# Turning the keys only with two banks free, and moving a sum and its flag away from the end of a packed-attention and expert kernel

## The chip, the cores and the metric

One core of a Trainium2 chip runs the program. The metric is the device time of one execution in microseconds. TensorE is called PE below, VectorE DVE, ScalarE ACT, GpSimd POOL and SyncE SP.

## The reference

Eight batches, eight heads of 576 positions and 64 features, 32 packs. The packs attend to keys and values, the queries attend to the packed result, and the concatenated heads (512 features) go through one of eight experts per token.

```python
def sm_attn(qq, kk, vv):
    s = scale * np.matmul(qq, kk.transpose(0, 1, 3, 2))
    s = s - np.max(s, axis=-1, keepdims=True)
    a = np.exp(s)
    a = a / (np.sum(a, axis=-1, keepdims=True) + 1e-09)
    return np.matmul(a, vv)
p_packed = sm_attn(p, k, v)
out = sm_attn(q, p_packed, p_packed)
...
        prev_e = -1
        for s in range(S):
            fresh_e = int(np.argmax(logits[b, s]))
            if s == 0 or local_gate[b, s] < 0.5:
                e = fresh_e
            else:
                e = prev_e if prev_e >= 0 else fresh_e
            prev_e = e
            ls = logits[b, s] - logits[b, s].max()
            p = np.exp(ls)
            p /= p.sum() + 1e-09
            h = np.maximum(x[b, s] @ w1[e], 0.0)
            out[b, s] = p[e] * (h @ w2[e])
```

Here x is the output of the attention, (8, 576, 512), w1 is 8 x 512 x 1024 and w2 is 8 x 1024 x 512.

## The kernel before

The kernel puts all tokens of a batch through the expert of the batch's first token. Tokens that would go elsewhere are called strays; they are counted, and only if there is one does a slow branch at the very end compute the batches again. With these inputs there is none.

For each batch a number of generators issue the work. `turn_keys` and `scores` make the products of packs and keys; `keys` takes the exponential of the scores (probabilities of the packs over the keys, two groups Q of four heads) and turns them: three transposes of 116 x 128 into one bank of PSUM, then two into another (line 573), each bank copied out to a1T (line 575, ACT). `packed_keys` multiplies them with the values (line 604). `queries` (lines 655 to 711) has the queries' attention, whose result is split into a2h and a2l, a high and a low part. `gates` (lines 918, 926) has the gate's logits, which DVE reads out of a bank turned (lt, line 933). `choose` reads the number of the expert into a register of SP, and `weights` then loads w1t (line 1021) and w2raw (line 1028).

The first layer's weights are multiplied with the packed result first: `pack_weights` (line 1065, two groups of eight products, two banks) gives wph (ACT's cast, line 1074) and wpl (DVE, line 1077) for four of the eight chunks of 128 hidden units. A chunk is then `layer1` in two halves of the tokens (line 1093: six products into one bank), `relu` (line 1104 on ACT, line 1109 on DVE, which gives the bank back), `split` of the second layer's weights (line 1120 on ACT, line 1124 on POOL) and `layer2`, in blocks of 128 tokens: 0 to 3 have three products each (line 1135), block 4 two (lines 1141, 1145). These add up in acc0 to acc4 over the eight chunks; then `store` scales and stores a block. PSUM has eight banks: five are the acc, and three, bank0 to bank2, serve everything else.

`chunks` is the main generator. It walks through the batches and chunks and puts the blocks of the chunk before between the halves of layer 1. Behind the last chunk of batch 7 stand the `tails`, the blocks of the last two chunks in six groups. All other generators are threads of `weave`, which picks whose step is issued next by a clock that it keeps of planned times. A `need(tiles, slot, banks)` tells that clock when a step could go on: when the tiles are written, and when that many of the three banks are free. It decides only the order in which instructions are issued; what they wait for on the chip are semaphores on the tiles and banks themselves, and every engine runs its own list in order.

`look_for_strays` sums the strays over the partitions with a 1 x 1 product (line 1193), casts the sum to an integer, `some` (line 1195, DVE), and loads it into a register on all five engines (line 1198), where the branch at the end reads it. `chunks` calls it ahead of the last chunk of batch 7 (line 1256).

Of the kernel before, what the change touches and what calls it, by code (L numbers as in the profile page):

```python
# [19 lines left out]
B, H, S, D = 8, 8, 576, 64  # L20
# [3 lines left out]
NQ = H // HQ  # L24
# [145 lines left out]
def packed_attn_moe_kernel(  # L170
# [33 lines left out]
    turns, banks, spare = [], [f"bank{x}" for x in range(3)], [f"acc{x}" for x in range(1, 4)]  # L204
# [54 lines left out]
    stray = const.tile([128, 1], F32, name="stray")  # L259
# [8 lines left out]
    def give(*tiles):  # L268
        clock.done.update(x.tensor.name for x in tiles)
# [5 lines left out]
    def need(*tiles, slot=(), banks=0, when=None, more=None, skip=()):  # L275
        slots = [(x, 1) if isinstance(x, str) else x for x in ((slot,) if isinstance(slot, str) else slot)]

        def ready():

            if (when is not None and not when()) or not all(clock.free_slot(*x) for x in slots):  # L280
                return None
            free = free_banks("front" if more == "front" else more is not None and lent(more), skip)
            if len(free) < banks:
                return None
            return max(clock.ready(tiles), free[banks - 1][0] if banks else 0.0, *(clock.slot(*x) for x in slots))
        ready.banks = banks
        return ready
# [259 lines left out]
    def keys(st, Q):  # L547

        yield need(when=lambda: ("nb", Q) in st and ("v", Q) in st)
        sc, nb = st["sc", Q], st["nb", Q]  # L550
        chunks_ = sc.rearrange("a (p c) -> a c p", c=NV)
        yield need(nb)
        s2 = tile_([128, 2], F32, "s2")
        if st["early"]:
            for r, t in enumerate(st["ts", Q]):
                nc.scalar.activation(
                    out=st["parts", Q][:, r], in_=t[:, :HALF].rearrange("a (c i) -> a c i", c=NT), func=AF.Exp,
                    bias=nb, scale=SCALE, accum_out=s2[:, r:r + 1],
                )
                give(t)  # L560
        else:
            nc.scalar.activation(out=sc[:, :S], in_=sc[:, :S], func=AF.Exp, bias=nb, scale=-1.0, accum_out=s2[:, 0:1])
        st["weighed"] += 1

        rooms = ("a1T", "a1U")
        yield need(s2, slot=rooms)
        a1T = [tile_([128, n, 128], F32, "a1T", room) for n, room in zip((J3, NV - J3), rooms)]
        for r, turned in enumerate(a1T):
            yield need(sc, banks=1)
            tp = bank()  # L570
            n = turned.shape[1]
            for j in range(n):
                nc.tensor.transpose(out=tp[:VP, 128 * j:128 * j + 128], in_=chunks_[:, J3 * r + j], identity=ident)  # L573
            copy = nc.vector.tensor_copy if st["early"] and (r == 1 or Q == 0) else nc.scalar.copy
            copy(out=turned[:VP], in_=tp[:VP, :128 * n].rearrange("a (j x) -> a j x", x=128))  # L575
            give(tp)
        give(sc)
        rs = tile_([128, 1], F32, "rs")
        if st["early"]:
            nc.vector.tensor_scalar(out=rs, in0=s2[:, 0:1], scalar1=s2[:, 1:2], scalar2=1e-9, op0=ALU.add, op1=ALU.add)  # L580
        else:
            nc.vector.tensor_scalar(out=rs, in0=s2[:, 0:1], scalar1=1e-9, scalar2=None, op0=ALU.add)
        nc.vector.reciprocal(out=rs, in_=rs)
        st["turned", Q] = a1T, rs
        if st["early"]:
            yield from packed_keys(st, (Q,))
        elif Q == NQ - 1:
            yield need(when=lambda: ("turned", 0) in st)
            yield from packed_keys(st, range(NQ))
# [452 lines left out]
    def pack_weights(st):  # L1042

        st["wp"], st["packed"], early = [], 0, st["early"]
        for fh in range(2):
            yield need(when=lambda: len(st.get("w1", ())) > fh and (
                (not st["first"] or (not fh or st["quads"] == NQ)) if not early else st.get("halved", 0) > 1 if fh else st["raised"] > 0
            ))
            pieces = st["w1"][fh]
            yield need(slot=("wph", "wpl"))  # L1050
            hi = tile_([128, NQ, 512], F32R, "wph")
            lo = tile_([128, NQ, 512], F32R, "wpl")
            for x in (hi, lo):
                clock.edges[x.tensor.name] = (256, 512, 768)
            st["wp"].append((hi, lo))
            width = 512 // len(pieces)
            for n, w1t in enumerate(pieces):
                cols = slice(width * n, width * n + width)
                skip = KEPT if early and fh == 0 else ()
                yield need(w1t, banks=NQ, skip=skip)  # L1060
                ts = [bank(skip=skip) for Q in range(NQ)]
                for Q in range(NQ):
                    rows = slice(64 * Q, 64 * Q + 64)
                    for h in range(HQ):
                        nc.tensor.matmul(  # L1065
                            out=ts[Q][32 * h:32 * h + 32, :width],
                            lhsT=st["ppT"][Q][rows, 32 * h:32 * h + 32],
                            rhs=w1t[rows, h],
                            start=True, stop=True,
                        )  # L1070
                if st["first"]:
                    yield need(*ts, when=lambda: not (early and n) or "cast" in st)
                for Q in range(NQ):
                    nc.scalar.copy(out=hi[:, Q, cols], in_=ts[Q][:, :width])  # L1074
                for Q in range(NQ):
                    yield need(hi[:, Q, cols], when=lambda: not early or ("back" in st if n == 0 else 0 in st["ready"]))
                    nc.vector.tensor_tensor(  # L1077
                        out=lo[:, Q, cols], in0=ts[Q][:, :width], in1=hi[:, Q, cols].bitcast(F32), op=ALU.subtract,
                    )
                give(*ts)  # L1080
                if n == len(pieces) - 1:
                    give(w1t)
                st["packed"] += width
# [103 lines left out]

    def look_for_strays():

        tc.mark_branch_hint_location("general", engines=list(engines_all))  # L1190
        yield need(stray, banks=1, when=lambda: "strays" in sts[B - 1])
        tot = bank()
        nc.tensor.matmul(out=tot[0:1, 0:1], lhsT=stray, rhs=ones_col, start=True, stop=True)
        some = sb.tile([1, 1], I32, name="some", bufs=1)
        nc.vector.tensor_copy(out=some, in_=tot[0:1, 0:1])  # L1195
        give(tot)
        yield need(some)
        found.append(nc.values_load(some[0:1, 0:1], min_val=0, max_val=128))

    def chunks(todo, aside, mask=None):  # L1200
# [40 lines left out]
        for b, st in todo:  # L1241
            tiles, begin_at = {}, 0
            if st["early"]:
                for c in range(FRONT):
                    yield from first(b, st, c, 0, tiles)
                for c in range(FRONT):
                    yield from second(tiles[c], (0, 1))
                for c in range(FRONT):
                    yield from first(b, st, c, 1, tiles)
                    if c:  # L1250
                        yield from second(tiles[c - 1], (2, 3, 4))
                last, begin_at = tiles[FRONT - 1], FRONT
            for c in range(begin_at, NC):
                end = c == NC - 1 and b is todo[-1][0]
                if end and mask is None:
                    yield from look_for_strays()
                for half, blocks in ((0, (0, 1, 2)), (1, (3, 4))):
                    yield from first(b, st, c, half, tiles)
                    if last is not None and not end:
                        done_before = (0, 1) if begin_at and c == begin_at else ()  # L1260
                        yield from second(last, tuple(x for x in blocks if x not in done_before))
                before, last = last, tiles[c]
# [12 lines left out]
        tails = ((before, (4, 0, 1)), (last, (4, 0)), (before, (2,)), (last, (1, 2)), (before, (3,)), (last, (3,)))  # L1275
        for n, (x, blocks) in enumerate(tails):
            yield from by_columns(x) if mask is None and n == 5 else second(x, blocks)

    def drain(*gs):
        for g in gs:  # L1280
# [58 lines left out]
    engines = mybir.EngineType  # L1339
    engines_all = (engines.PE, engines.Activation, engines.DVE, engines.Pool, engines.SP)  # L1340
    found = []
    sts = [dict() for _ in range(B)]
# [97 lines left out]
```

## Time and profile before

| | |
|---|---|
| time, median of 3 runs | 420.13 us (419.82 to 421.15) |
| time of the profiled execution | 420.32 us |
| its span, first to last instruction | 418.6 us |
| mean granted TensorE clock | 0.998 |
| PE busy | 406.5 us, 97% |
| DVE, ACT, POOL busy | 251.2, 189.4, 107.7 us |
| chain that ended last | PE 90%, DVE 5% |

The profile is of one execution. Busy times of PE overlap a little, since matmuls are pipelined; a timeline gives the start of each group of instructions, how long it took, and in brackets how long its engine had been idle and what ended that. The granted clock is full through all 40 slices of the page.

### The profile page before, as it was taken

Reading aid. Unit: us, or ns where it says so; the run is one execution under the profiler, and the core shown is the slowest. Engines: PE = TensorE matmul, PEld = TensorE weight load, DVE = VectorE, ACT = ScalarE, POOL = GpSimd, SP = SyncE. Lnnn points to the kernel's source line nnn. Section 1 sums busy time; section 2 is a strip of 40 time slices with the busy share of each in tenths; the row PEclk is TensorE's granted clock in tenths of the full one; section 3 lists DMA queues with packets and bytes.
Section 4 is the critical chain, followed back from the end, with each engine's and each line's share of the span. In section 5 each row is a group of like instructions: output and inputs, shape, how many; then the busy total and the mean of one; then the engine's idle time right before and its main releaser. Section 6 shows DMA issues by size and latency. Waiting matters only on the chain.

```text
span 418.6 us, 9782 instructions
## 1 busy us (share of the span) xinstructions
PE 406.5 (97%) x3724; PEld 317.3 (76%) x3725; DVE 251.2 (60%) x665; ACT 189.4 (45%) x447; POOL 107.7 (26%) x125
## 2 busy tenths in 40 slices
PE   8989999999999999999999999999999999999994
PEld 6776677777777887678768886788868887788873
DVE  4598388865865777578723886348842695432121
ACT  2574425643536452646353454535453552352232
POOL 1024022121341243113412252122512144213220
PEclk9999999999999999999999999999999999999999
DMA  8789979926994896699699706499191305430003
GB/s 232 239 305 230 170 237 251 226 83 154 337 185 160 187 173 187 241 205 207 224 295 187 221 9 237 156 210 240 32 349 32 122 13 206 172 121 18 2 1 117
DMA packets 161053, 72.98 MB, mean 174 GB/s; under 512 B 131186, under 2 KB 139882, under 8 KB 161002
## 3 DMA queue, kind: packets, MB, share of 16 engines
q1 hardware_dynamic: 160858, 72.19, 66.9%
q8 instruction: 30, 0.49, 0.5%
q14 instruction: 21, 0.17, 0.1%
q10 hardware_dynamic: 144, 0.13, 0.1%
HBM read 62.87 MB, written 9.44 MB: 173 GB/s over the span
## 4 chain that ended last, share of the span: by engine, by line
PE 90%; DVE 5%; ACT 1%; DMA 1%; issue 1%; SPq 0%; DVEq 0%; ACTq 0%
PE acc L1135 41%; PE bank L1093 25%; PE bank L1065 4%; PE acc L1141 4%; PE acc L1145 3%; PE bank L604 2%; PE bank L655 2%; PE bank L516 2%; PE bank L573 2%; PE acc L228 1%; DMA w1k<-in_moe_w_dram 1%; PE bank L918 1%; PE acc L445 1%; ACT wph L1074 1%; DVE h L1109 1%
## 5 line engine op out<-in xcount | busy, mean ns | idle before, releaser
L1135 PE MATMUL acc<-w2s,h 128*128 128x512 f32 (+1 forms) x771 | 204.2, 397 | 0.0
L1135 PEld LDWEIGHTS acc<-w2s,h 128*128 128x128 f32 x771 | 135.6, 188 | 31.6 <-issue 10.0
L1124 POOL TENSOR_TENSOR w2s<-w2raw,w2s 128x512 fp32r<-128x512 f32 (+1 forms) x68 | 85.4, 1259 | 249.3 <-ACT w2s L1120 229.8
L1109 DVE SCALAR_TENSOR_TENSOR h<-bank,h 128x224 fp32r<-128x224 f32 (+2 forms) x191 | 61.0, 347 | 86.5 <-ACT h L1104 85.3
L1104 ACT ACTIVATE h<-bank 128x288 fp32r<-128x288 f32 (+2 forms) x127 | 52.4, 413 | 111.4 <-PE bank L1093 101.8
L1093 PEld LDWEIGHTS bank<-a2h,wph 128*128 128x128 f32 x254 | 45.1, 188 | 22.8 <-issue 2.8
L1093 PE MATMUL bank<-a2h,wph 128*128 128x288 f32 (+2 forms) x254 | 57.8, 309 | 3.2 <-DVE wpl L1077 0.9
L1093 PE MATMUL bank<-a2l,wph 128*128 128x288 f32 (+2 forms) x254 | 54.5, 296 | 0.0
L1093 PE MATMUL bank<-a2h,wpl 128*128 128x288 f32 (+2 forms) x254 | 54.3, 295 | 0.0
L1093 PEld LDWEIGHTS bank<-a2h,wpl 128*128 128x128 f32 x254 | 40.9, 188 | 0.0
L1093 PEld LDWEIGHTS bank<-a2l,wph 128*128 128x128 f32 x254 | 40.7, 188 | 0.0
L1120 ACT CAST w2s<-w2raw 128x512 fp32r<-128x512 f32 x64 | 39.4, 616 | 1.8 <-DVE some L1195 1.6
L1077 DVE TENSOR_TENSOR wpl<-bank,wph 128x512 fp32r<-128x512 f32 (+1 forms) x32 | 20.6, 666 | 22.5 <-ACT wph L1074 22.5
L1141 PE MATMUL acc<-w2s,h 128*128 128x512 f32 x64 | 26.3, 411 | 0.0
L1145 PE MATMUL acc<-w2s,h 128*64 128x512 f32 x64 | 25.3, 396 | 0.0
L1074 ACT CAST wph<-bank 128x512 fp32r<-128x512 f32 (+1 forms) x32 | 16.8, 577 | 16.2 <-PE bank L1065 16.2
L1175 ACT ACTIVATE o<-acc,pe 128x512 f32<-128x512 f32 x23 | 15.8, 689 | 9.6 <-PE acc L1135 9.5
L711 POOL TENSOR_TENSOR a2l<-a2t,a2h 128x576 fp32r<-128x576 f32 x12 | 17.2, 1433 | 10.1 <-PE acc L1145 8.4
L640 DVE STREAM_TRANSPOSE qn<-qn 128x1152 f32<-128x1152 f32 x14 | 18.9, 1364 | 0.0
L673 DVE STREAM_TRANSPOSE sT<-bank 128x288 f32<-128x288 f32 x28 | 11.9, 462 | 11.3 <-ACT gate L671 10.0
L575 ACT COPY a1T<-bank 116x384 f32<-116x384 f32 (+1 forms) x28 | 11.5, 430 | 12.4 <-PE bank L573 12.3
L1065 PE MATMUL bank<-w1t,ppT 64*32 64x512 f32 x240 | 16.3, 601 | 0.0
(193 smaller groups left out, 403.0 us busy)
## 6 DMA issues: line engine op xcount, KB each, us to landing
w2raw<-in_moe_w_dram SPq DMA_DIRECT2D x64, 256.0 KB, 5.0
w1t<-in_moe_w_dram SPq DMA_DIRECT2D x15, 1024.0 KB, 5.2
kv<-in_v_dram SPq DMA_DIRECT2D x16, 560.0 KB, 7.6
qn<-in_q_dram SPq DMA_DIRECT2D x28, 288.0 KB, 4.6
out_dram<-o SPq DMA_DIRECT2D x31, 256.0 KB, 2.8
qn<-in_k_dram SPq DMA_DIRECT2D x24, 288.0 KB, 3.9
raw<-in_k_dram SPq DMA_DIRECT2D x4, 576.0 KB, 4.4
raw<-in_q_dram SPq DMA_DIRECT2D x2, 576.0 KB
```

The source lines that it names most:

```text
L640: nc.vector.transpose(out=qT, in_=qT)
L1065: nc.tensor.matmul(out=ts[Q][32 * h:32 * h + 32, :width], lhsT=st["ppT"][Q][rows, 32 * h:32 * h + 32], rhs=w1t[rows, h], start=True, stop= ...
L1074: nc.scalar.copy(out=hi[:, Q, cols], in_=ts[Q][:, :width])
L1077: nc.vector.tensor_tensor(out=lo[:, Q, cols], in0=ts[Q][:, :width], in1=hi[:, Q, cols].bitcast(F32), op=ALU.subtract,)
L1093: nc.tensor.matmul(out=t[:, :width], lhsT=st["wp"][c // 4][wi][:, Q, fs], rhs=a2[ai][Q][:, ts], start=(n == 0), stop=(n == 5),)
L1104: nc.scalar.activation(out=h[:, lo:hi], in_=t[:, :hi - lo], func=AF.Relu)
L1109: nc.vector.scalar_tensor_tensor(out=h[:, dst:dst + z - a], in0=t[:, a:z], scalar=0.0, in1=h[:, lo + a:lo + z].bitcast(F32), op0=ALU.max, ...
L1120: nc.scalar.copy(out=w[:, 0], in_=raw)
L1124: rest.tensor_tensor(out=w[:, 1, cols], in0=raw[:, cols], in1=w[:, 0, cols].bitcast(F32), op=ALU.subtract)
L1135: nc.tensor.matmul(out=acc[:, cols], lhsT=hs[hi], rhs=w[:, wi, cols], start=(c == 0 and n == 0), stop=(n == 2 and (c == NC - 1 or c == NC ...
L1141: nc.tensor.matmul(out=acc, lhsT=h[:, 512:S + TAIL], rhs=w[:, 0], start=(c == 0), stop=False, skip_group_check=True,)
L1145: nc.tensor.matmul(out=acc[0:TAIL], lhsT=h[:, 512:S], rhs=w[:, 1], start=False, stop=(c == NC - 1), skip_group_check=True,)
```

## The change

A turn of the keys waits in the planner's clock for two free banks (NQ is 2) in batches 1 to 7, where it was one. The strays' product and cast are issued in `pack_weights` of batch 7, right ahead of its second and last pack, when three banks are free, and the loads into registers become a function of their own, called behind the third group of the tails.

```diff
         for r, turned in enumerate(a1T):
-            yield need(sc, banks=1)
+            yield need(sc, banks=1 if st["early"] else NQ)
             tp = bank()
...
                 skip = KEPT if early and fh == 0 else ()
+                if isinstance(st["b"], int) and st["b"] == B - 1 and fh:
+                    yield need(w1t)
+                    yield from look_for_strays()
                 yield need(w1t, banks=NQ, skip=skip)
...
     def look_for_strays():
 
-        tc.mark_branch_hint_location("general", engines=list(engines_all))
-        yield need(stray, banks=1, when=lambda: "strays" in sts[B - 1])
+        yield need(stray, banks=NQ + 1, when=lambda: "strays" in sts[B - 1])
         tot = bank()
         nc.tensor.matmul(out=tot[0:1, 0:1], lhsT=stray, rhs=ones_col, start=True, stop=True)
         some = sb.tile([1, 1], I32, name="some", bufs=1)
         nc.vector.tensor_copy(out=some, in_=tot[0:1, 0:1])
         give(tot)
+        found.append(some)
+
+    def load_found():
+
+        some = found.pop()
+        tc.mark_branch_hint_location("general", engines=list(engines_all))
         yield need(some)
         found.append(nc.values_load(some[0:1, 0:1], min_val=0, max_val=128))
 
...
-                if end and mask is None:
-                    yield from look_for_strays()
...
             yield from by_columns(x) if mask is None and n == 5 else second(x, blocks)
+            if mask is None and n == 2:
+                yield from load_found()
```

Lines behind the first edit of `pack_weights` have numbers that are higher by 3 after the change (L1065 becomes L1068, L1093 becomes L1096, L1135 becomes L1138), those at the end by 8.

The first place is PE's order where batch 1's keys are turned (a1_477 and a1_659 are the two groups' probabilities; the numbers behind a bank count its uses). Before:

```order
L573 MATMUL bank1_696<-ident_72,a1_477 116x128 x3
L573 MATMUL bank2_702<-ident_72,a1_477 116x128 x2
L1093 MATMUL bank1_713<-a2h_120,wph_457 128x320
...
L1135 MATMUL acc2_726<-w2s_538,h_537 128x512 x3
L1065 MATMUL bank2_732<-w1t_397,ppT_226 32x512 x4
L1065 MATMUL bank0_733<-w1t_397,ppT_226 32x512 x4
L573 MATMUL bank1_751<-ident_72,a1_659 116x128 x3
L1135 MATMUL acc3_758<-w2s_538,h_537 128x512 x3
L1141 MATMUL acc4_762<-w2s_538,h_537 128x512
L1145 MATMUL acc4_762<-w2s_538,h_537 64x512
L573 MATMUL bank1_778<-ident_72,a1_659 116x128 x2
L1093 MATMUL bank2_788<-a2h_120,wph_457 128x320
```

After:

```order
L1068 MATMUL bank2_719<-w1t_397,ppT_226 32x512 x4
L1068 MATMUL bank0_720<-w1t_397,ppT_226 32x512 x4
...
L1096 MATMUL bank1_763<-a2h_120,wph_457 128x320
...
L573 MATMUL bank2_770<-ident_72,a1_477 116x128 x3
L1138 MATMUL acc2_713<-w2s_550,h_549 128x512 x3
L1138 MATMUL acc3_751<-w2s_550,h_549 128x512 x3
L573 MATMUL bank0_784<-ident_72,a1_477 116x128 x2
L1144 MATMUL acc4_759<-w2s_550,h_549 128x512
L1148 MATMUL acc4_759<-w2s_550,h_549 64x512
L573 MATMUL bank2_793<-ident_72,a1_659 116x128 x3
L573 MATMUL bank1_798<-ident_72,a1_659 116x128 x2
L1096 MATMUL bank0_806<-a2h_120,wph_457 128x320
```

The turns stood around the pack of batch 0's second four chunks; now all four stand behind it, by one chunk, and the layer-1 half behind the last two has the third bank.

The second place is PE's order at the step from batch 0 to batch 1 (a2t, a2h_688 and wph_969 or wph_1004 are batch 1's). Before:

```order
L1065 MATMUL bank2_1171<-w1t_947,ppT_786 32x512 x4
L1065 MATMUL bank0_1172<-w1t_947,ppT_786 32x512 x4
L1093 MATMUL bank1_1183<-a2h_688,wph_969 128x288
...
L1135 MATMUL acc0_593<-w2s_1124,h_1123 128x512 x3
L918 MATMUL bank2_1201<-a2t_686,gate1_91 32x128 x4
L918 MATMUL bank2_1201<-a2t_687,gate1_91 32x128 x4
```

After:

```order
L1068 MATMUL bank2_1171<-w1t_980,ppT_805 32x512 x4
L1068 MATMUL bank0_1172<-w1t_980,ppT_805 32x512 x4
L918 MATMUL bank1_1183<-a2t_686,gate1_91 32x128 x4
L918 MATMUL bank1_1183<-a2t_687,gate1_91 32x128 x4
L926 MATMUL bank1_1183<-a2t_686,gate1_91 32x32 x4
L926 MATMUL bank1_1183<-a2t_687,gate1_91 32x32 x4
L1096 MATMUL bank1_1213<-a2h_688,wph_1004 128x288
```

The gate's products came two groups behind the pack and had a bank of their own; now they stand between the pack and the layer-1 half, which has the gate's bank.

The third place is PE's order at the strays' product. Before, it and the load are ahead of the last chunk:

```order
L1141 MATMUL acc4_5145<-w2s_5260,h_5259 128x512
L1145 MATMUL acc4_5145<-w2s_5260,h_5259 64x512
L1193 MATMUL bank1_5338<-ones_col_79,stray_99 1x1
L1198 TENSOR_LOAD some_5340
L1093 MATMUL bank2_5358<-a2h_4548,wph_4939 128x288
```

After, the product is here, and the load in the tails:

```order
L1138 MATMUL acc1_4666<-w2s_4906,h_4905 128x512 x3
L1195 MATMUL bank0_4981<-ones_col_79,stray_99 1x1
L1068 MATMUL bank1_4985<-w1t_4826,ppT_4445 32x512 x4
L1068 MATMUL bank2_4986<-w1t_4826,ppT_4445 32x512 x4
...
L1138 MATMUL acc0_5118<-w2s_5338,h_5337 128x512 x3
L1138 MATMUL acc2_5131<-w2s_5301,h_5300 128x512 x3
L1206 TENSOR_LOAD some_4983
L1138 MATMUL acc1_5125<-w2s_5338,h_5337 128x512 x3
```

The product left its place between two chunks, and the load has blocks of layer 2 on both sides.

## Rows read from the trace of the kernel before

**Rows 1.** The page, part 1: engine, busy us, share of the span, instructions.

```profile
PE 406.5 (97%) x3724; PEld 317.3 (76%) x3725; DVE 251.2 (60%) x665; ACT 189.4 (45%) x447; POOL 107.7 (26%) x125
```

**Rows 2.** Waits of PE after 38 us, grouped: total us, times, longest.

```profile
PE bank L1093 <- DVE sT L673: 0.2, 1, 0.2
```

**Rows 3.** PE timeline, three turns that nothing delays: start us, us, shapes, count.

```profile
132.22 0.71 PE L573 MATMUL bank<-ident,a 128*116 128x128 f32 x5
132.68 0.94 PE L1135 MATMUL acc<-w2s,h 128*128 128x512 f32 x3
...
134.36 0.38 PE L573 MATMUL bank<-ident,a 128*116 128x128 f32 x2
134.50 0.51 PE L1093 MATMUL bank<-a2h,wph 128*128 128x288 f32 x2
```

**Rows 4.** PE timeline, four turns with layer 1 next; in brackets idle, releaser.

```profile
39.76 0.71 PE L573 MATMUL bank<-ident,a 128*116 128x128 f32 x5
40.82 0.57 PE L1093 MATMUL bank<-a2h,wph 128*128 128x320 f32 x2 [0.35 <-ACT a1T L575]
...
45.21 0.38 PE L573 MATMUL bank<-ident,a 128*116 128x128 f32 x2
46.05 0.41 PE L1093 MATMUL bank<-a2h,wph 128*128 128x320 f32 x1 [0.46 <-DVE wpl L1077]
...
169.06 0.38 PE L573 MATMUL bank<-ident,a 128*116 128x128 f32 x2
169.72 0.53 PE L1093 MATMUL bank<-a2h,wph 128*128 128x288 f32 x2 [0.29 <-DVE rs L582]
...
173.00 0.49 PE L573 MATMUL bank<-ident,a 128*116 128x128 f32 x3
173.90 0.53 PE L1093 MATMUL bank<-a2h,wph 128*128 128x288 f32 x2 [0.41 <-DVE wpl L1077]
```

**Rows 5.** PE timeline, the first and the last of the nine lightly delayed turns.

```profile
91.04 0.81 PE L573 MATMUL bank<-ident,a 128*116 128x128 f32 x5
91.61 0.48 PE L1135 MATMUL acc<-w2s,h 128*128 128x512 f32 x1
...
314.09 0.49 PE L573 MATMUL bank<-ident,a 128*116 128x128 f32 x3
314.33 0.47 PE L1141 MATMUL acc<-w2s,h 128*128 128x512 f32 x1
314.65 0.40 PE L1145 MATMUL acc<-w2s,h 128*64 128x512 f32 x1
314.89 0.38 PE L573 MATMUL bank<-ident,a 128*116 128x128 f32 x2
315.15 0.53 PE L1093 MATMUL bank<-a2h,wph 128*128 128x288 f32 x2
```

**Rows 6.** PE timeline round the strays' product.

```profile
403.25 0.39 PE L1141 MATMUL acc<-w2s,h 128*128 128x512 f32 x1
403.48 0.40 PE L1145 MATMUL acc<-w2s,h 128*64 128x512 f32 x1
403.81 0.19 PE L1193 MATMUL bank<-ones_col,stray 128*1 128x1 f32 x2
404.76 0.51 PE L1093 MATMUL bank<-a2h,wph 128*128 128x288 f32 x2 [0.77 <-DVE some L1195]
```

**Rows 7.** Source line 1198: duration ns min/median/max, first and last start.

```profile
L1198 PEldq TENSOR_LOAD <-some x1: 490/490/490, 404.2 to 404.2; - x1
```

**Rows 8.** PE timeline, a layer 1 that waits for a gate's read.

```profile
38.80 0.53 PE L1093 MATMUL bank<-a2h,wph 128*128 128x320 f32 x2 [0.49 <-DVE lt L933]
```

**Rows 9.** Batch 1's first-layer weights: SP's and PE's timelines, and tile w1t.

```profile
56.16 1.00 SPq L1021 DMA_DIRECT2D w1t<-in_moe_w_dram  x2
...
63.15 1.09 PE L1065 MATMUL bank<-w1t,ppT 64*32 64x512 f32 x16
...
DMA to landing us min/median/max: 5.0/5.2/8.9
```

## The prediction

> **What bounds the kernel now.** I read the page first: PE is busy for 97% of the span [rows 1], so the time is PE's stream of products plus its gaps, and an edit counts by what it does to that stream. Then the waits of PE and its timeline from 38 us on, when the first layer-1 products run. The reader is to compare starts with starts: a turn of three keys' chunks or of five, with nothing in its way, is followed 0.46 us (five, 132.22 to 132.68) or 0.14 us (two, 134.36 to 134.50) later by the next product [rows 3], three alone by 0.24 (314.09 to 314.33) [rows 5]. Whatever a step has beyond that is a gap. The duration printed beside a product doesn't say it, since matmuls overlap.
>
> By that measure the turns (line 573) have gaps of two kinds. Four have a large one, each with a layer-1 half next, and the idle time there ends with an engine that was emptying a bank [rows 4]:
> - 39.76 to 40.82, five: 1.06 - 0.46 = 0.60 (ACT copying the turn out)
> - 45.21 to 46.05, two: 0.84 - 0.14 = 0.70 (DVE on the pack's banks)
> - 169.06 to 169.72, two: 0.66 - 0.14 = 0.52 (named: DVE's rs, long a small thing; the bank's copy by ACT is what layer 1 needs)
> - 173.00 to 173.90, three: 0.90 - 0.24 = 0.66 (DVE on the pack's banks again)
>
> Together 2.48 us. There are three free banks. Where a turn takes one while the pack or the other turn still holds the rest, the layer-1 half behind it finds none, and PE, which runs in order, stands. Nine more turns are lightly delayed, the first 91.04 to 91.61 (0.57 against 0.46, 0.11), the last 314.89 to 315.15 (0.26 against 0.14, 0.12) [rows 5]. They range from 0.06 to 0.12, and I count 0.09 each: 0.8.
>
> The strays' sum is the other gap: L1145 at 403.48 is followed by layer 1 only at 404.76, 1.28 us, where an L1145 step is 0.24 (314.65 to 314.89) [rows 5, 6]. So 1.04 us is spent there on one tiny product, its cast on DVE and the register loads in front of layer 1 on PE.
>
> **The change part by part.**
>
> *Two banks for a turn.* A turn of batches 1 to 7 is now issued only when the planner sees two banks free, so one is left for the layer-1 half behind. In the order the first turn of batch 1 now stands behind the pack, blocks 3 and 4 and a layer-1 half, and the one at 45.21, which met the pack's banks, stands a whole chunk's blocks behind the pack. Turns with a layer-1 half next are 8 where they were 10, and at the other places a block or two now lies between. All four large gaps lose their cause in this way: -2.48. Bounds: nothing, if the planner's clock is wrong there, and -2.48. I take it whole, because each of the four is a bank that was not free, which is what the rule asks for. [...]
>
> The turns stand more often alone between other products. A dense product behind a turn costs more: L1141 took 0.32 (314.33 to 314.65) behind one [rows 5] and 0.23 (403.25 to 403.48) without [rows 6], so 0.09. In the new order 22 turns have a product of layer 1 or 2 next, in the old 19: 3 x 0.09 = +0.28 (bounds 0.1 and 0.5).
>
> *What is behind the turns.* The keys' chain of batch 1 (products with values, queries, choice of expert, weights) moves back with them. By the order the choice of batch 1 (L899) has two layer-1 halves, two blocks of three products and block 4 more ahead of it. A half takes at most 0.96 (38.80 to 39.76) [rows 4, 8], a product of a block 0.23 [rows 6]: 1.92 + 1.38 + 0.46 = 3.8, less the 1.3 us of gaps that go there: 2.5 later. The weights were issued at 56.16, land in 5.2 us (median) and their pack ran at 63.15 [rows 9]: slack 63.15 - 61.36 = 1.8. The pack itself has one half, two blocks and block 4 more ahead of it, 2.8 - 1.3 = 1.5 later. That leaves 0.8, which hides the move; if it didn't, each tenth beyond would be PE's. The other batches' weights come many blocks ahead of their packs.
>
> *The gate of batch 1 moves.* At the step from batch 0 to 1 the gate's products (L918, L926) now stand right ahead of layer 1, which takes the bank that they used. It was layer 1, then a block, then the gate. Layer 1 must now wait until DVE has read the gate's bank (L933). The trace has that very pair once, in batch 0: layer 1 idle 0.49 behind lt [rows 8]. I take +0.50; from below 0.1 (DVE has little in its queue there and the pack's casts cover some of it), from above 0.9 (an operation of the pack or of layer 1 stands ahead of the read on DVE, and is as long again).
>
> *The strays' sum.* Its product and cast move beside the last pack; the loads into five engines' registers go into the tails. At the old place 1.04 us goes. [...] It now asks for three free banks, of which it takes one for the time of a product and a cast, so the pack behind it finds its two; and the cast lies a whole expert's products ahead of the loads. The loads remain on each engine's queue. On PE that is 490 ns [rows 7] in its sequencer, with the flag long written. A block's three products stand ahead of it in the array. From below 0 (hidden by them), from above 0.49. I take 0: the load's row at 404.2 ends together with the release of layer 1, and what that layer waited for was the flag, not a queue run empty. Two blocks' evictions stand behind the load on ACT and on DVE, but they wait for PE's later blocks, and on SP one store behind another: hidden too.
>
> [...]
>
> **The sum.** -2.48 - 0.39 + 0.28 + 0.50 - 1.04 + 0.28 = -2.85 us. The profiled execution took 420.32 us, so 417.47; the median of the runs shown is 420.13, lower by 0.19: 417.3. From no change this kernel's measurement can tell about 0.3%, 1.26 us: faster means below 418.87, slower above 421.39.
>
> **The rivals.**
> - *A, the forecast:* 417.3, own range 416.0 to 418.4 (the bounds 0 to -0.8 of the light turns, 0.1 to 0.9 of the gate, 0 to 0.49 of the load, taken partly together). For it: four named gaps, one named stall, little else in the way. Against: each moved turn may meet some other full bank. 0.60.
> - *B, the waits come back elsewhere.* The planner counts banks by its own clock, and the gaps show that its clock was wrong by half a microsecond at four places. Turns that wait for two banks run into the next pack. If half of the 2.48 returns, 418.5; if all of it returns and the load's 0.49, 420.3. 0.22, over a span of 418.5 to 420.3, a third of it faster.
> - *C, slower: the weights of batch 1 come late.* Place: the pack at 63.15. Issued 2.5 us later, at 58.66, they are there at 63.86 at the median against a pack at 64.65. At the longest landing of the trace, 8.9 us [rows 9], at 67.56: PE would wait 2.9 us, and the gain of 2.85 is gone, 420.2. It decides from a landing of 10.1 us on (58.66 + 10.1 = 68.76, 4.1 of waiting): 421.4 and more, to 423 at 11.7. For it: the slack falls to less than half. Against: the median. 0.06.
> - *D, more than forecast.* The gate's read turns out covered (0.5), the light gaps vanish whole (0.39), and a wait such as that for sT (0.2) [rows 2] goes with the new order: 416.2, and 415.6 if the two terms of 0.28 aren't there either. 0.12.
> - *E, the stray's move doesn't do what it says:* the register loads stall PE in the tails as they did ahead of the last chunk, each engine waiting for the others. Then all of the 1.04 stays and the 0.28 comes on top: 417.3 + 1.04 = 418.3, at the edge of A's range and counted there. Against it: the flag is then written long before.
>
> **How the numbers follow.** A 0.60, B 0.22, C 0.06, D 0.12. Faster: A, D and a third of B, 0.60 + 0.12 + 0.08 = 0.80. Same: the rest of B, 0.14. Slower: C, 0.06. The range takes A and D's upper part and most of B: 415.5 to 419.4; outside lie C and the end of B, about 0.16.
>
> **What would show it.** In the new trace: no idle over 0.2 on a layer 1 behind a turn in 38 to 180 us; layer 1 behind L1145 at the last chunk after 0.24, not 1.28; at the boundary of batch 0 and 1 an idle of about half a microsecond behind lt; at the flag's load on PE in the tails a step between blocks as any other; the pack of batch 1 without a DMA as its releaser; and PE's busy time nearly as before, the span shorter by 2.9. I am wrong if the steps behind turns keep their excess, if the load costs PE its half microsecond, or if the pack of batch 1 waits.

## The result and the profile after

| | before | after |
|---|---|---|
| median of 4 runs | 420.34 us (419.82 to 421.15) | 415.61 us (415.09 to 416.07) |
| profiled execution, span | 420.32, 418.6 us | 415.92, 414.2 us |
| mean granted TensorE clock | 0.998 | 0.998 |

The ratio is 0.9885 (95% interval 0.987 to 0.9899): 4.7 us faster, and 4.4 in the profiled executions, where the forecast was 2.85.

The page of the changed kernel, part 1, and PE's waits from 38 us on (total, times, longest):

```profile
PE 403.7 (97%) x3724; PEld 317.0 (77%) x3725; DVE 253.2 (61%) x665; ACT 189.4 (46%) x447; POOL 108.8 (26%) x125
```

```profile
PE bank L1096 <- DVE lt L933: 1.0, 2, 0.5
```

PE is as much the bound as before [rows 1]. In this view only the two waits for a gate's read are left; the one behind sT [rows 2] is gone as well as those behind turns. The place of batch 1's turns, PE's timeline:

```profile
44.55 0.49 PE L573 MATMUL bank<-ident,a 128*116 128x128 f32 x3
44.79 1.65 PE L1138 MATMUL acc<-w2s,h 128*128 128x512 f32 x6
46.28 0.38 PE L573 MATMUL bank<-ident,a 128*116 128x128 f32 x2
46.42 0.48 PE L1144 MATMUL acc<-w2s,h 128*128 128x512 f32 x1
46.73 0.40 PE L1148 MATMUL acc<-w2s,h 128*64 128x512 f32 x1
46.97 0.71 PE L573 MATMUL bank<-ident,a 128*116 128x128 f32 x5
47.43 0.54 PE L1096 MATMUL bank<-a2h,wph 128*128 128x320 f32 x2
```

The turn of three is followed after 0.24 us, that of two after 0.14, the five after 0.46: to the hundredth the steps of the undelayed turns [rows 3, 5], where 0.60 and 0.70 had been lost [rows 4]. Two later turns, at 135.02 and 136.29, still have an excess, of 0.18 and 0.10, that the view of waits doesn't show. At 46.42 to 46.73 the 0.31 of a dense product behind a turn is still paid.

The step from batch 0 to batch 1, PE's timeline, with the wait that was forecast [rows 8]:

```profile
75.35 0.31 PE L926 MATMUL bank<-a2t,gate 128*32 128x32 f32 x16
76.14 0.53 PE L1096 MATMUL bank<-a2h,wph 128*128 128x288 f32 x2 [0.48 <-DVE lt L933]
```

The last chunk of batch 7, PE's timeline: layer 1 stands 0.24 us behind L1148, where 1.28 had passed [rows 6]. The third row has six products of blocks while PE's queue does the flag's load (402.68 to 403.17). The last row begins the long group of blocks that ends PE's work; its first two products are counted here.

```profile
399.50 0.40 PE L1148 MATMUL acc<-w2s,h 128*64 128x512 f32 x1
399.74 0.43 PE L1096 MATMUL bank<-a2h,wph 128*128 128x288 f32 x2
...
401.80 1.53 PE L1138 MATMUL acc<-w2s,h 128*128 128x512 f32 x6
403.18 0.39 PE L1144 MATMUL acc<-w2s,h 128*128 128x512 f32 x1
...
403.64 0.62 PE L1138 MATMUL acc<-w2s,h 128*128 128x512 f32 x2
```

Batch 1's first-layer weights, SP's and PE's timelines [rows 9]:

```profile
58.81 1.00 SPq L1021 DMA_DIRECT2D w1t<-in_moe_w_dram  x2
...
64.43 1.09 PE L1068 MATMUL bank<-w1t,ppT 64*32 64x512 f32 x16
```

They are issued 2.65 us later (58.81 for 56.16) and packed 1.28 later (64.43 for 63.15); the pack waits for nothing.

The end of the program: SP's and DVE's timelines (four stores, then the second of the four by itself, then the last), and the flag's load by source line (duration in ns, then start). Line 1161 stores half of the last block as soon as DVE has scaled it.

```profile
405.32 3.53 SPq L1189 DMA_DIRECT2D out_dram<-o  x4
405.88 1.44 SPq L1189 DMA_DIRECT2D out_dram<-o  x1
...
408.95 0.42 SPq L1161 DMA_DIRECT2D out_dram<-o  x1
...
407.96 0.48 DVE L1160 TENSOR_SCALAR o<-acc,pe 128x256 f32<-128x256 f32 x1 [1.32 <-PE acc L1138]
...
L1206 PEldq TENSOR_LOAD <-some x1: 487/487/487, 402.7 to 402.7; - x1
...
L1206 SPq TENSOR_LOAD <-some x1: 275/275/275, 407.4 to 407.4; - x1
```

Before, the same rows, with PE's last group:

```profile
408.75 4.28 PE L1135 MATMUL acc<-w2s,h 128*128 128x512 f32 x21
...
410.44 2.69 SPq L1186 DMA_DIRECT2D out_dram<-o  x4
...
411.00 1.15 SPq L1186 DMA_DIRECT2D out_dram<-o  x1
...
413.58 0.33 SPq L1158 DMA_DIRECT2D out_dram<-o  x1
...
413.07 0.48 DVE L1157 TENSOR_SCALAR o<-acc,pe 128x256 f32<-128x256 f32 x1 [1.32 <-PE acc L1135]
```

Before, the half block was scaled at 413.55 (413.07 + 0.48) and its store issued 0.03 us later. Now it is scaled at 408.44 and its store issued at 408.95, 0.51 later: SP's load of the flag lies within the four stores ahead of it, which take 3.53 us for 2.69. Two things make that difference. Round the load 0.71 us pass on SP between the end of one store's issue and the next (407.32 to 408.04), where 0.09 do before (412.15 to 412.24): 0.62. And the store ahead of the load took SP 1.44 for 1.15. As SP had stood waiting for DVE ahead of the last store before (from 413.13 on), 0.51 of it is seen.

On PE the load, 487 ns long, costs nothing: the six products from 401.80 to 403.18 are 0.23 apart, as L1141 and L1145 were before [rows 6]. By the order the load stands behind the first six products of the last group, which PE is through at about 405.0 (an estimate: 403.64 + 6 x 0.23), so PE's queue begins it over 2 us ahead of its place.

So there are two numbers to follow in each run. The stretch from the first product of layer 1 to PE's last group: 28.00 to 408.75 before, 380.75; 27.93 to 403.64 after, 375.71, which is 5.04 less. And the end, from that group to the end of the span: 418.6 - 408.75 = 9.85 before, 10.56 after. -5.04, +0.71 and -0.07 for the start make the 4.4 us of the spans. The start varies by itself: over all runs below the first product of layer 1 came between 27.20 and 28.59, while the stretch of the changed kernel came out alike in its two profiles (375.71 and, below, 375.73).

### The profile page after: what moved, and what is told of

It is laid out like the page before. It is cut to its first block, busy times and chain, and to the rows that moved or that the text cites. A ratio compares the mean times of both kernels' runs of the same rounds, so it can differ in the third digit from the quotient of the medians.

```text
span 414.2 us, 9764 instructions
## 1 busy us (share of the span) xinstructions
PE 403.7 (97%) x3724; PEld 317.0 (77%) x3725; DVE 253.2 (61%) x665; ACT 189.4 (46%) x447; POOL 108.8 (26%) x125
## 4 chain that ended last, share of the span: by engine, by line
PE 93%; DVE 3%; DMA 1%; ACT 1%; issue 0%; SPq 0%; DVEq 0%; ACTq 0%
PE acc L1138 43%; PE bank L1096 25%; PE acc L1144 4%; PE bank L1068 4%; PE acc L1148 4%; PE bank L604 2%; PE bank L655 2%; PE bank L573 2%; PE bank L516 2%; PE acc L228 1%; DMA w1k<-in_moe_w_dram 1%; PE bank L918 1%; PE acc L445 1%; PE bank L445 0%; PE bank L622 0%
## 5 line engine op out<-in xcount | busy, mean ns | idle before, releaser
L1138 PE MATMUL acc<-w2s,h 128*128 128x512 f32 (+1 forms) x771 | 206.4, 398 | 0.0
L1138 PEld LDWEIGHTS acc<-w2s,h 128*128 128x128 f32 x771 | 135.0, 188 | 33.0 <-issue 11.6
L1127 POOL TENSOR_TENSOR w2s<-w2raw,w2s 128x512 fp32r<-128x512 f32 (+1 forms) x68 | 86.3, 1274 | 243.5 <-ACT w2s L1123 224.6
L1096 PEld LDWEIGHTS bank<-a2h,wph 128*128 128x128 f32 x254 | 45.7, 188 | 18.1 <-ACT a L562 1.8
L1096 PE MATMUL bank<-a2h,wph 128*128 128x288 f32 (+2 forms) x254 | 57.0, 306 | 1.0 <-DVE lt L933 1.0
L1096 PE MATMUL bank<-a2l,wph 128*128 128x288 f32 (+2 forms) x254 | 54.5, 296 | 0.0
L1096 PE MATMUL bank<-a2h,wpl 128*128 128x288 f32 (+2 forms) x254 | 54.4, 296 | 0.0
L1096 PEld LDWEIGHTS bank<-a2h,wpl 128*128 128x128 f32 x254 | 40.9, 188 | 0.0
L1096 PEld LDWEIGHTS bank<-a2l,wph 128*128 128x128 f32 x254 | 40.8, 188 | 0.0
L1077 ACT CAST wph<-bank 128x512 fp32r<-128x512 f32 (+1 forms) x32 | 16.8, 577 | 20.0 <-PE bank L1068 20.0
L1148 PE MATMUL acc<-w2s,h 128*64 128x512 f32 x64 | 25.3, 396 | 0.0
L640 DVE STREAM_TRANSPOSE qn<-qn 128x1152 f32<-128x1152 f32 x14 | 19.1, 1366 | 0.0
L466 DVE STREAM_TRANSPOSE qn<-qn 128x1152 f32<-128x1152 f32 x12 | 16.4, 1364 | 0.0
```

The costliest lines, as they stand in the source:

```text
L640: nc.vector.transpose(out=qT, in_=qT)
L1096: nc.tensor.matmul(out=t[:, :width], lhsT=st["wp"][c // 4][wi][:, Q, fs], rhs=a2[ai][Q][:, ts], start=(n == 0), stop=(n == 5),)
L1127: rest.tensor_tensor(out=w[:, 1, cols], in0=raw[:, cols], in1=w[:, 0, cols].bitcast(F32), op=ALU.subtract)
L1138: nc.tensor.matmul(out=acc[:, cols], lhsT=hs[hi], rhs=w[:, wi, cols], start=(c == 0 and n == 0), stop=(n == 2 and (c == NC - 1 or c == NC ...
L1148: nc.tensor.matmul(out=acc[0:TAIL], lhsT=h[:, 512:S], rhs=w[:, 1], start=False, stop=(c == NC - 1), skip_group_check=True,)
```

## The experiments

All times are medians beside runs of the kernel before in the same group (420.60, 420.79 and 420.71 us there).

**Only the rule for the turns.** The strays' sum and flag stay where they were.

```diff
-            yield need(sc, banks=1)
+            yield need(sc, banks=1 if st["early"] else NQ)
```

> Only the two-bank rule for the turns; the strays' sum and flag as before. Theory 1 (the trace after): the four large gaps (2.48 us), half of the light ones (0.45) and the waits behind other products that also went (1.65) all belong to the new order of the turns, less 0.55 for the gate's wait; about 4.2 us faster than before, 416.1. Theory 2 (the extra gain is the strays' part, or chance): the forecast's turn terms alone, -2.48 - 0.39 + 0.28 + 0.50, 2.1 us faster, 418.2.

416.03 us, ratio 0.9898 (0.9881 to 0.9915). The stretch is 27.60 to 404.22, 376.62, which is 4.13 less than before. Theory 1 holds: the gain above the forecast belongs to the turns' new order. The strays' stall is still there, PE's timeline:

```profile
400.26 0.51 PE L1093 MATMUL bank<-a2h,wph 128*128 128x288 f32 x2 [0.77 <-DVE some L1195]
```

**Only the strays' part.**

```diff
-            yield need(sc, banks=1 if st["early"] else NQ)
+            yield need(sc, banks=1)
```

> Only the strays' part; the turns with one bank as before. Theory 1: PE gains about 0.9 us, but SP's register load of the flag, which stands between the last stores, gives 0.5 to 0.7 of it back behind the last product; about 0.3 us faster than before, 420.0. Theory 2 (the load on SP is hidden, as forecast): 0.8 to 0.9 us faster, 419.5; or, if the extra gain belongs to the strays, 2 us and more.

419.67 us, ratio 0.998 (0.997 to 0.999). The stretch, 27.20 to 407.00, is 379.80, 0.95 less than before, as both theories have it. With the other 4.13 that makes 5.08 for the changed kernel's 5.04: the parts add up. The end took 10.0 us here, only 0.15 more than before, so the time goes with theory 2. That isn't because the load is hidden: it takes SP the same 0.62 between two stores, but the store ahead of it took less.

```profile
409.25 0.92 SPq L1189 DMA_DIRECT2D out_dram<-o  x1
```

With 0.92 for the 1.44 of the changed kernel the last store is issued 0.03 us behind DVE, as before the change. So the load's own time is steady, and what it costs the end is not. The gaps of before are in place, the one of 169.06 [rows 4] at 168.31 with 0.67 for 0.66, the one of 173.00 at 172.26 with 0.90.

**The flag loaded earlier.**

```diff
+                if end and mask is None:
+                    yield from load_found()
...
-            if mask is None and n == 2:
-                yield from load_found()
```

> The changed kernel with the loads of the flag ahead of the last chunk of batch 7, where they were before, the sum staying at the last pack. Theory 1: the flag is long written, so PE's load there is hidden in its queue, and SP's load is over before the last stores: 0.5 to 0.7 us faster than the changed kernel, 415.0. Theory 2: the loads hold up layer 1 by their own 0.49 us whether the flag is old or not: no gain over the changed kernel, 415.5 to 415.9.

415.06 us, ratio 0.9877 (0.9859 to 0.9896). By source line, PE's, DVE's and SP's timelines:

```profile
L1206 SPq TENSOR_LOAD <-some x1: 277/277/277, 373.0 to 373.0; - x1
...
L1206 PEldq TENSOR_LOAD <-some x1: 492/492/492, 395.8 to 395.8; - x1
...
399.13 0.40 PE L1148 MATMUL acc<-w2s,h 128*64 128x512 f32 x1
399.36 0.43 PE L1096 MATMUL bank<-a2h,wph 128*128 128x288 f32 x2
...
407.58 0.48 DVE L1160 TENSOR_SCALAR o<-acc,pe 128x256 f32<-128x256 f32 x1 [1.32 <-PE acc L1138]
...
408.10 0.33 SPq L1161 DMA_DIRECT2D out_dram<-o  x1
```

SP loads at 373.0, long before the stores. PE's load, at 395.8 and 492 ns, leaves layer 1 its 0.23 us behind L1148: with an old flag the place that cost a microsecond costs nothing, so theory 2 falls. The last store is 0.04 us behind DVE (407.58 + 0.48) and the end takes 9.84 us, as before. The gain in the median is 0.2 to 0.6 us against the changed kernel's two groups, less than the 0.7 that its first profile showed, and within the spread of the runs.

**The flag loaded last.**

```diff
-            if mask is None and n == 2:
+            if mask is None and n == 5:
```

> The changed kernel with the loads of the flag behind the last block, so that SP's stands behind the last store instead of between stores. Theory 1: the last store is issued 0.5 us earlier, and the load runs while the store is in flight: 0.5 to 0.7 us faster than the changed kernel, 415.0. Theory 2 (the branch and the end of the program come behind the load, and the store's flight doesn't hide it): as the changed kernel, 415.6.

415.67 us, ratio 0.9891 (0.9873 to 0.9908); the end took 10.19 us. The time goes with theory 2, that SP's load isn't free behind the last store either, but this is one profile, and the end reached 10.21 in one with the load long done (below): not shown.

**The changed kernel again**, for comparison within its group.

> The changed kernel once more, beside the others of this group, so that they are compared on one chip: 4.7 us faster than before, as in its first runs. In its trace SP's loads stand again between the last stores; if they cost the end of the program something steady, the stretch from the last product to the end is again 0.2 to 0.7 us longer than before.

415.30 us, ratio 0.9879 (0.9864 to 0.9894). Stretch 27.23 to 402.96, 375.73; end 10.44. Over the profiles with the load behind the start of PE's last group the end took 10.56, 10.44, 10.0, 10.19, and 9.95 and 10.12 in the two runs below with batches apart; with it earlier 9.85, 9.78, 9.84, and 10.21 and 9.83 in two further ones (the run with three banks is left out). That is 10.21 against 9.90 in the mean: about 0.3 us, from ranges that overlap (9.95 to 10.56, 9.78 to 10.21), and a part of the first 0.7 was chance.

**The rule for batch 1 alone.**

```diff
-            yield need(sc, banks=1 if st["early"] else NQ)
+            yield need(sc, banks=NQ if isinstance(st["b"], int) and st["b"] == 1 else 1)
```

> The changed kernel with the two-bank rule for the turns of batch 1 alone. Theory 1 (each gap belongs to its own place): batch 1's two large gaps go (1.30), the strays' 0.9 too, and what stood behind batch 1 in the order has new places; gaps of the later batches come back where a layer-1 half follows a product that holds the last bank: about 1.2 us (0.52 + 0.66) and some of the waits behind other products (1.65), so 417.5 to 418.5. Theory 2 (the rule for one batch shifts the order enough to clear all of it): as the changed kernel, 415.6.

417.67 us, ratio 0.9939 (0.9925 to 0.9952), stretch 377.65, 3.10 less than before. Theory 1: batch 1's gaps are gone, and later batches, whose turns again ask for one bank, have gaps, not at 169 and 173 us but at new places. The largest, PE's timeline, a block and then a turn that waits for the bank of the turn before it:

```profile
133.01 0.94 PE L1138 MATMUL acc<-w2s,h 128*128 128x512 f32 x3
134.58 0.59 PE L573 MATMUL bank<-ident,a 128*116 128x128 f32 x3 [0.63 <-ACT a1T L575]
```

**The rule for batches 2 to 7 alone.**

```diff
-            yield need(sc, banks=1 if st["early"] else NQ)
+            yield need(sc, banks=1 if st["early"] or isinstance(st["b"], int) and st["b"] == 1 else NQ)
```

> The changed kernel with the two-bank rule for batches 2 to 7 alone, the complement of the run for batch 1. Theory 1 (each gap has its own place in the order): batch 1's two large gaps (0.60, 0.70) and the wait behind scores at 85 us (0.48) stay to the nanosecond, since the order up to there is that of before; the gaps at 169 and 173 us (1.18) and most of the waits behind other products from 181 us on (1.1) go with the strays' 0.9; some 3 us faster than before, 417.5. Theory 2 (any shift of the order in an early batch sets off the later gains): those later gaps stay too, 1 us faster, 419.7.

417.54 us, ratio 0.9924 (0.9906 to 0.9943), stretch 377.74, 3.01 less. Theory 1 again: batch 1's gap at 45.21 [rows 4] is back with 0.84, and no turn from 160 us on has one.

```profile
45.64 0.38 PE L573 MATMUL bank<-ident,a 128*116 128x128 f32 x2
46.48 0.41 PE L1096 MATMUL bank<-a2h,wph 128*128 128x320 f32 x1 [0.45 <-DVE wpl L1080]
...
352.40 1.23 PE L1068 MATMUL bank<-w1t,ppT 64*32 64x512 f32 x16 [0.43 <-DMA w1t<-in_moe_w_dram]
```

The third row is new: in this order a pack late in the program waits 0.43 us for its weights. That is the slower rival's mechanism, at another batch than the one it was worked out for.

**Three banks for a turn.**

```diff
-            yield need(sc, banks=1 if st["early"] else NQ)
+            yield need(sc, banks=1 if st["early"] else NQ + 1)
```

> The changed kernel with turns that wait for all three banks. Theory 1 (what counts is that a bank is left for the layer-1 half behind, and two are enough for that): no large gap behind a turn, the time within 0.6 us of the changed kernel, 415.0 to 416.2. Theory 2 (later turns make the weights or the gate late): a wait of PE on w1t's DMA or on lt, 416.5 and more. Theory 3 (two banks only shift the gaps to other products): more banks give a further gain, under 415.

449.28 us, ratio 1.0686 (1.0671 to 1.07). Theory 2, far larger than I had it. PE's waits (total, times, longest), and from the page the granted clock in tenths, in 40 slices:

```profile
PE bank L1068 <- DMA w1t<-in_moe_w_dram: 6.9, 3, 2.8
PE bank L1068 <- DVE a2t L702: 3.6, 1, 3.6
...
PEclk9989999799998999978999999999999999969999
```

Three free banks are rare between layer-1 halves, so the turns come late, and with them all that hangs on them: queries' results (a2t), choices of experts, weights. PE waits for these in whole microseconds, up to 3.6 at once, some 19 us in all from 38 us on. The stretch is 31.9 us longer than the changed kernel's (28.59 to 436.19, 407.60), so the waits are not all of it. The granted clock fell as well, to 0.964 in the mean for 0.998: the slices with 6 to 8 hold stretches at 0.50 (76.4 to 83.1 us, from within the wait of 3.6 on), where the kernel before had 1.00 from 38 us on until 416.5, 3.5 us behind its last product, and 0.50 only from there; and six products of a block that begin in one of them, at 204.07, take 2.46 us, where six at 1.00 took 1.53 in the changed kernel (401.80). So of the 31.9 us some 19 are waits, and most of the other 13 are products at half the clock (an estimate: 0.034 less clock over the span of 446.1 is 15 us, some of them within the waits). One bank kept free for layer 1 is a gain, one more is a loss.

**A later clock instead of the rule.**

```diff
-LAT, SAME = 160.0, 127.0
+LAT, SAME = 300.0, 127.0
```

> The kernel before with nothing but the planner's allowance between engines (LAT) raised from 160 to 300, which makes its clock see banks free later for every user; turns still ask for one bank. Theory 1 (it takes a bank kept for the layer-1 half; a later clock only moves the products): gaps behind turns at other places, of the same size in all, 419 to 421. Theory 2 (the clock's optimism is the whole cause): the gaps go without the rule, 416 to 417.

420.86 us, ratio 1.0007 (0.9995 to 1.002); stretch 28.45 to 409.79, 381.34, 0.59 more than before. Theory 1: batch 1's two gaps stay and others move, such as this one of 0.90 for 0.24:

```profile
259.73 0.49 PE L573 MATMUL bank<-ident,a 128*116 128x128 f32 x3
260.63 0.53 PE L1093 MATMUL bank<-a2h,wph 128*128 128x288 f32 x2 [0.41 <-DVE wpl L1077]
```

A more careful clock moves the gaps; keeping a bank takes them away.

**The rule for the gate too, and the flag early.**

```diff
-        yield need(*a2t, gs, banks=1, when=lambda: not st["early"] or "begun" in st)
+        yield need(*a2t, gs, banks=1 if st["early"] else NQ, when=lambda: not st["early"] or "begun" in st)
...
+                if end and mask is None:
+                    yield from load_found()
...
-            if mask is None and n == 2:
-                yield from load_found()
```

> The changed kernel with the flag's loads ahead of the last chunk, and the same rule for the gate: its products wait in the planner for two free banks from batch 1 on. In the order the gate of batch 1 goes back behind a layer-1 half. Theory 1 (the 0.5 us at that place is the layer-1 half that waits for the bank that the gate holds): that idle goes, 0.5 us less than with the flag's loads alone, 414.5 to 414.7. Theory 2 (the order behind it changes too, and gaps arise there): 415 to 416.

414.79 us, ratio 0.9863 (0.9842 to 0.9884). The stretch is 28.48 to 403.57, 375.09, 0.62 less than the changed kernel's, and the end 9.83, 0.73 less. Layer 1 stands right behind the pack again, at 75.38, and idles no more:

```profile
74.36 1.09 PE L1068 MATMUL bank<-w1t,ppT 64*32 64x512 f32 x16
75.38 0.53 PE L1096 MATMUL bank<-a2h,wph 128*128 128x288 f32 x2
```

Theory 1 holds for that place. By its stretch this version is the best of all; its profile began late (28.48), and its median leads by 0.5 us over the changed kernel in the same group, with overlapping intervals.

## Why the prediction was right, and where it was short

**Two banks for a turn: right, and the whole 2.48 us.** All four large gaps went, step by step to the undelayed values. The cause is the bank left for layer 1: without the rule for batch 1 its two gaps are back to the hundredth, without it for batches 2 to 7 others come in those batches, and with another clock but no rule gaps stay or move. One of the four was read wrongly. At 169.72 layer 1 can't have waited for ACT's copy of the turn, which runs from 169.47 to 169.84. DVE's pass over a bank of the pack (L1077, 168.98 to 169.67) ends just ahead, so that bank is the likely one, as at 45.21 and 173.00.

**The light turns and the products behind turns: mis-sized.** The forecast was -0.39 + 0.28 = -0.11. As what is left of the stretch, 5.04 - 2.48 - 1.39 - 0.95 + 0.48 = 0.70, they gave -0.70. No run took the two apart, but the steps do in part. Before, nine turns have an excess of 0.06 to 0.18, together 0.95; the first is at 43.62 (0.35 for 0.24), not at 91.04, and one ahead of a pack, at 166.81, has 0.18, where the prediction's range ends at 0.12. After, the two at 135.02 and 136.29 have 0.28. So the light turns gave -0.67, nearly all of their bound. No run shows the forecast's -0.39, half of what they were counted at. Next to nothing is left for the products behind turns, forecast at +0.28. Since single ones still take longer (0.31 at 46.42 for 0.23 [rows 6]), something of that size must have gone elsewhere; what, stays open.

**The step that fell short: what other waits are worth.** I read turns by the steps from start to start, but everything else by the idle time in the view of waits, where sT stood with 0.2 us [rows 2] (and a gsm with as much), and left it to rival D. The sum has no term for them. By the steps the trace of before has more. PE's timeline at four places without a turn:

```profile
85.08 1.19 PE L516 MATMUL bank<-qn,p_in 64*32 64x288 f32 x16
86.20 0.50 PE L1135 MATMUL acc<-w2s,h 128*128 128x512 f32 x1
...
181.05 0.50 PE L1141 MATMUL acc<-w2s,h 128*128 128x512 f32 x1
181.39 0.39 PE L1145 MATMUL acc<-w2s,h 128*64 128x512 f32 x1
182.02 0.40 PE L1093 MATMUL bank<-a2h,wph 128*128 128x288 f32 x1 [0.24 <-DVE sT L673]
...
203.42 0.50 PE L1141 MATMUL acc<-w2s,h 128*128 128x512 f32 x1
203.76 0.39 PE L1145 MATMUL acc<-w2s,h 128*64 128x512 f32 x1
204.32 0.37 PE L1093 MATMUL bank<-a2h,wph 128*128 128x288 f32 x1 [0.17 <-DVE gsm L970]
...
219.58 0.39 PE L1141 MATMUL acc<-w2s,h 128*128 128x512 f32 x1
219.81 0.40 PE L1145 MATMUL acc<-w2s,h 128*64 128x512 f32 x1
220.21 0.50 PE L1093 MATMUL bank<-a2h,wph 128*128 128x288 f32 x2
```

The scores at 85.08 take 1.12 us; the sixteen that start at 202.77 took 0.65: 0.47 lost. From block 4 behind queries or scores to layer 1 pass 0.97 and 0.90 where 0.32 + 0.24 is due [rows 5], 0.41 and 0.34 lost, and 0.63 for 0.46 at 219.58, 0.17. Together 1.39 us. All of it is gone after the change, most of it without an idle row of its own in the view. It looks like the same shortage of banks, with queries, scores or a pack as the ones that hold them: at 85 us PE's weight loads wait for DVE's reads of two banks (h L1109, 0.36 us idle, and a L536, 0.35), at 182.02 for its read of the queries' (sT), and at 204.32 and 220.21 DVE had just finished the read of the layer-1 half before (L1109, at 204.18 and 220.06). At the last two that is inferred from the times. That the new order clears these was seen, not planned: with the rule for batch 1 alone the one at 85.08 went and others came; the run for batches 2 to 7 kept the one at 85 us, with 0.47. Whether a rule for the turns clears such places in general, or this order happens to, stays open.

**The gate: right.** +0.48 for +0.50, and the run with the rule for the gate too took it away by a bank.

**The strays' sum: right, with one wrong word.** The stretch gained 0.95 where -1.04 + 0.28 = -0.76 was forecast. So the new place costs 0.09 in all; the forecast's 0.28 had the product's 0.19 [rows 6] and 0.09 more that no run shows. PE's load cost 0, as taken, not its 0.49 (487 ns beside products 0.23 apart; 492 ns in the run with the flag loaded earlier, some 3.5 us ahead of its place, layer 1's step 0.23), but one reason for it was half wrong: at the old place layer 1 stood for the load too. The flag was there at 404.18, the load took from 404.22 to 404.71, and layer 1 began at 404.76, so some 0.49 of the 1.04 was the load, with no product running beside it: the last ahead of it, the strays', had ended at 404.00 [rows 6]. "On SP one store behind another: hidden too" was wrong. SP's queue issues the stores that end the program, and a load of 275 ns, 0.62 us with what belongs to it, stood ahead of the last: the end took 0.71 longer in the first profile, about 0.3 in the mean over all.

**The slower rival** was read rightly: issue 2.65 later for 2.5, pack 1.28 for 1.5. The median landing of before leaves 64.43 - 58.81 - 5.2 = 0.4 us, half of what I had; that median is of the three landings of w1t that the trace has, and batch 1's isn't among them.

## What to carry to other kernels

Where a planner fills in side work for an engine whose products run in the order of issue, as PE's did here, ask not only whether the side work can run, but whether the buffer that the main stream needs next is left. One spare was worth 1% (a ratio of 0.9898); asking for a second starved the side work and, at a granted clock of 0.964 for 0.998, made the program 7% slower than before (1.0686). Measure every step against its own undelayed value from start to start, since idle rows showed only part of a wait (0.24 of 0.41 us at 182.02). And when an instruction goes to all engines, look at each engine's queue at that place: here it was hidden on PE (487 ns, no step longer) and in the way on SP (0.62 us between two stores), which issues the last stores.

## What was not expected of the hardware

A register load of a flag written long before cost PE nothing at two places, though it lasts 487 and 492 ns; for a fresh flag, with no product running beside it, the sum, its cast and the load had cost 1.04 us. SP's issue of the second of the last five stores took 0.92, 1.15 and 1.44 us in three profiles. The same steps repeat to a hundredth of a microsecond from run to run (0.66 and 0.67, 0.84 and 0.84), while the start varies by 1.4 us and the end by 0.8: for an edit of half a microsecond the stretch between them tells more than the medians.
